# Attention beside a gated feed-forward network: the value products of two key tiles in one block, feed-forward products in six places of two rounds

## The chip, the cores and the metric

The kernel runs on one core of a Trainium2 chip. The core has five engines with queues of their own: TensorE (PE in the profile; its weight loads are shown apart as PEld), VectorE (DVE), ScalarE (ACT), GpSimd (POOL) and SyncE (SP), which here issues the DMAs. Each engine works through its own list of instructions in order and waits on semaphores for the others. TensorE writes only to PSUM, whose eight banks of 128 x 512 fp32 numbers have to be emptied by VectorE or ScalarE before they can be written again.

The metric is the device time of one execution in microseconds. Of the kernel before there are three runs: 1801.42, 1802.56 and 1802.78 us; the median is 1802.56.

## The reference

The input is one sequence of 2048 tokens with 512 features, all in fp32.

```
xn = layernorm(x)
q, k, v = split(xn @ wqkv)              # 32 heads of 16
p  = softmax(q @ k.T / sqrt(16))        # per head, 2048 x 2048
s  = (p @ v) @ wo
g  = silu(((xn @ w_gate) * (xn @ w_up)) @ w_down)   # inner width 1792
out = x + s * g
```

## The kernel before, in words

**Precision.** Most products run on TensorE as fp32r, a rounded fp32. To keep the accuracy, an operand is split into a high part and a low remainder, and a product is the sum of three (high times high, high times low, low times high). The value products alone run in plain fp32, which the chip does as two passes, so that each is two matmul records in the trace.

**Units, rounds, key tiles.** The attention is cut into 32 units: a group of four heads (eight groups) and a chunk of 512 query tokens (four chunks). A unit goes through 16 key tiles of 128 keys. One key tile of one unit is a *round*; the main loop runs over 512 rounds, `n` from 0 to 511, and `kt` is the key tile. In a round, for each of the four heads `j`:

- `expo` (line 603) multiplies the key tile by the queries into a PSUM tile `t` (keys on the partitions, 512 queries). Two further rows of the contraction carry the negated maximum of each query, so ScalarE's exponential (line 605) gives the unnormalised weights `e` in SBUF directly.
- `score` (line 578) makes the plain scores `s` (queries on the partitions, 512 keys) for a unit 21 rounds ahead (`LEAD`), and VectorE takes their maximum (line 580, `mx`). That is what `expo` of a later unit needs. The last 21 rounds have no scores.

The heads sit in the lower and the upper 64 partitions in turn: `t` of head `j` and `s` of head `j ^ 1` use different halves of the array's rows and run side by side. A `t` and its `s` are called a *pair* below; a round has four pairs, two rounds have eight.

**Value products.** `pv` (line 614) multiplies the `e` tiles of a round by the values and a column of ones (which gives the softmax's denominator), for its four heads in four strips of 32 output partitions of one PSUM bank, `pv`, accumulated over the 16 key tiles. They use all 128 rows of the array and 32 of its columns each, where the other products use 64 rows and 128 columns. After the last key tile, `finish` transposes, divides and sends the result out. The value products of a round are placed after the pairs of the next round.

**Feed-forward and projections.** The projections of queries and keys for later heads, the feed-forward network and the output projection are cut into products that run between the rounds' other work. `pair` (lines 256 to 277) makes two such outputs at a time, in two PSUM banks (`misc`), with the contraction cut into the lower and upper 64 rows: at each step one matmul of each half (lines 269 and 273), 24 or 30 steps in all, in two halves `k` = 0 and 1. It yields `k` and the number of steps ahead of each half, and then once a step. Between the halves ScalarE makes a one-element copy, `look`, that fixes the order. After a gate/up product ScalarE copies the gate out (`g`, line 374), VectorE multiplies it with the other output (`h`, line 376), and some steps later ScalarE and GpSimd split that into `hh` and `hl` (lines 334 and 335).

A `Filler` doles these steps out. It takes the step count of a half and the number of rounds that `spread` gives it (from `FFN_ROUNDS` = 484 rounds over all `SLOTS`), and in each round `part` issues an equal share of what is left. In the loop `part` is called once a round, after the second pair. So a round of TensorE's list is: pair, pair, four to six feed-forward steps, pair, pair, then the value products of the round before.

**What sets the order.** TensorE, ScalarE and VectorE keep exactly the order in which the program issues instructions (`manual_schedule`, `ORDERED`). `soon(n, fn)` puts small operations off by `n` calls of `step()`, which comes once after each pair. GpSimd and SyncE are ordered by a planner after the first 18 rounds.

**Buffers.** PSUM: `st` 2 banks for `t`, `s` 3, `pv` 1, `misc` 2 (`BUFS`). SBUF: 12 tiles for `e` (`EBUFS`), three for a unit's queries.

Of the kernel before, what the change touches and what calls it, by code (L numbers as in the profile page):

```python
# [21 lines left out]
NT = S // P  # L22
# [7 lines left out]
VCOLS = (H - 1) * VW + 32  # L30
THIRDS = [range(0, 5), range(5, 10), range(10, 14)]
LEAD = 21
FFN_ROUNDS = 484
SLOTS = 24 * (NC * (NG // 2 - 1) + 1) + 36 * NF * NC
SPLIT_ROUNDS = 4
EBUFS = 12
# [12 lines left out]
def body(ctx, tc, x, wqkv, wo, wg, wu, wd, out):  # L49
# [4 lines left out]
    class Tied:  # L54
# [3 lines left out]
        def __init__(self, engine):  # L58
            self.engine, self.last = engine, None
# [13 lines left out]
    def dma(dst, src):  # L73
        sync.dma_start(dst, src)
# [36 lines left out]
    def banks_of(bufs):  # L111
        stack = ExitStack()
        fst["ps"] = stack.enter_context(tc.tile_pool(name="ps" + "".join(bufs), bufs=1, space=PSUM, reuse_waits="tile")), bufs
        return stack

    def psum(tag, name):
        ps, bufs = fst["ps"]
        return ps.tile([P, 512], F32, tag=tag, name=name, bufs=bufs[tag])
# [290 lines left out]
    def o_split(c, tiles):  # L409

        for d, (oh, ol) in enumerate(tiles):
            heads = 8 if c < NC - 1 or d < ND - 1 else 4
            n = heads * DH
            raw = (wtile(("w1r", "w0r")[d]).rearrange("p d q -> p (d q)") if d < 2 else
                   fst["fp"].tile([P, D], F32, name="wdr", bufs=2))
            dma(raw[:n], OD[c][8 * d:8 * d + heads, 0:DH])
            pool.tensor_copy(oh[:n], raw[:n])
            pool.tensor_tensor(ol[:n], raw[:n], oh[:n], op=OP.subtract)
        ops[c] = now[0], tiles

    def small_tiles():

        return [[wtile(n + k).rearrange("p d q -> p (d q)") for k in "hl"] for n in ("w1", "w0") for _ in range(2)]

    def prepare():

        done = [(NG - 1) * NC + c in finished for c in range(NC)]
        if 0 not in ops:
            if done[0] and "w" in fst:
                o_split(0, small_tiles())  # L430
        for c in (1, 2):
            if c not in ops and done[c] and ("big", c) in fst:
                h, l = fst["big", c]
                o_split(c, [(h[:, d], l[:, d]) for d in range(ND)])
        if 3 not in ops and "first" in fst:
            o_split(3, small_tiles())
# [103 lines left out]
    NU = NG * NC  # L540
# [6 lines left out]
    def load_q(i):  # L547
        g, c = divmod(i, NC)
        QS[i] = q = keep.tile([P, 2, 512], F32R, name="qs", bufs=3)
        MX[i] = keep.tile([P, 4, 4, 4], F32, name="mx", bufs=2)  # L550
        for e in range(2):
            dmar(q[64 * e:64 * e + KB], two(QD[g // 2][c][64 * (g % 2):64 * (g % 2) + 64], e))

    def load_k(g, cs=range(NC)):
        heads = slice(64 * (g % 2), 64 * (g % 2) + 64)
        for e in range(2):
            k = ks[g % 2][64 * e:64 * e + KB]
            if g < 2:
                for c in cs:
                    dmar(k[:, :, c * 512:(c + 1) * 512], two(KD[0][c][heads], e))  # L560
            else:
                dmar(k, two(KD[g // 2][heads], e))
# [45 lines left out]
    def pv(i, kt, es):  # L608
        g = i // NC
        if kt == 0:  # L610
            fst["pv"] = psum("pv", f"pv{i}")
        for j in range(4):
            h0 = (4 * g + j) * VW
            nc.tensor.matmul(fst["pv"][32 * j:32 * j + 32], V[:, kt, h0:h0 + 32], es[j],  # L614
                             start=kt == 0, stop=kt == NT - 1)

    def finish(i):

        g, c = divmod(i, NC)
        tr = keep.tile([P, 16, 32], F32, name="tr", bufs=1)  # L620
        tn = tr.rearrange("p b e -> p (b e)")
        nc.vector.transpose(tn, fst["pv"])
        yield
        rc = keep.tile([P, 16, 1], F32, name="rc", bufs=1)
        nc.vector.reciprocal(rc, tr[:, :, DH:DH + 1])
        late = i >= NU - NC
        (nc.vector if late else pool).tensor_tensor(on[:, :, 0:DH], tr[:, :, 0:DH], rc.to_broadcast([P, 16, DH]),
                                                         op=OP.mult)
        for _ in range(1 if late else 5):
            yield  # L630
        nc.vector.transpose(tn, on.rearrange("p b e -> p (b e)"))
        if i == NU - 1:
            fst["tn"] = tn
            return
        dma(OD[c][4 * g:4 * g + 4], tn)
        finished.add(i)
# [111 lines left out]
    def filler(wq0):  # L748
        yield from proj_pair(0, [(wq0, 0, 2), (wq0, 0, 3)])
        for m in range(1, NG // 2):  # L750
            wk, wq = fst.get(("qk", m)) or (qk_weights(m, 1), qk_weights(m, 0))
            for c in range(NC):
                yield from proj_pair(m, [(wk, 1, c), (wq, 0, c)])
                if m == 1 and c:
                    after = fst["high"].ins.name
                    for n, src in enumerate((xh, xl)):
                        put = sync.dma_start(XD[c][n].bitcast(F32), src[c].bitcast(F32))
                        tc.add_manual_dep(put.ins, after, BEHIND, reason="not before the first exponentials")
                if m == NG // 2 - 1 and c == NC - 2:
                    nxt = gu_weights(0)  # L760
        flush()
        qkv.close()
        fst["fp"] = ffp.enter_context(tc.tile_pool(name="ffn", bufs=1, reuse_waits="tile"))
        yield from ffn(nxt)
# [3 lines left out]
    heads = []  # L768

    def step_small(q):  # L770
        if q and next(q[0], 1):
            q.pop(0)

    class Filler:


        def __init__(self, gen, rounds):
            self.gen, self.rounds = gen, rounds
            self.left = self.parts = 0
            self.done = False  # L780

        def fetch(self):
            v = next(self.gen, self)
            if v is self:
                self.done = True
            elif v:
                self.left, self.parts = v[1], self.rounds(v[1])

        def part(self):
            if not self.left and not self.done:  # L790
                self.fetch()
            if self.left:
                n = -(-self.left // self.parts)
                for _ in range(n):
                    next(self.gen)
                self.left -= n
                self.parts = max(1, self.parts - 1)
                if not self.left:
                    self.fetch()

    cum = [0]

    def spread(n):
        a = cum[0]
        cum[0] += n
        return max(1, round(cum[0] * FFN_ROUNDS / SLOTS) - round(a * FFN_ROUNDS / SLOTS))

    prev = None
    with tc.manual_schedule(engines=ORDERED):
        with banks_of(EARLY_BUFS):  # L810
            fil = Filler(filler(early()), spread)
        ctx.enter_context(banks_of(BUFS))
        for n in range(NU * 16):
            now[0] = n
            Tied.on = n < 18
            i, kt = divmod(n, 16)
            g, c = divmod(i, NC)
            si, sr = divmod(n + LEAD, 16)
            if kt == 8 and i + 2 < NU:
                load_q(i + 2)  # L820
            if kt == 0 and g + 1 < NG and c == 1:
                load_k(g + 1)
            es = []
            for j in range(4):
                es.append(expo(i, kt, j))
                if si < NU:
                    score(si, sr, j ^ 1)
                step()
                if j == 1:
                    prepare()  # L830
                    if fil.done:
                        fil = Filler(ending(), lambda n: 2)
                    fil.part()
            if sr == 15 and si < NU:
                maxima(si, 8 if si < NU - 1 else 4)
            step_small(heads)
            if kt % 4 == 2:
                soon(2, lambda: step_small(later))
            if prev is None:
                run(fst["v"])  # L840
            else:
                pv(*prev)
                if prev[1] == NT - 1:
                    heads.append(finish(prev[0]))
                    step_small(heads)
            prev = i, kt, es
        pv(*prev)
        run(finish(NU - 1))
        flush()
        last_heads()  # L850
        while fil.left or not fil.done:
            now[0] += 1
            prepare()
            fil.part()
            flush()
# [17 lines left out]
```

## Time and profile before

| | |
|---|---|
| median of three runs | 1802.56 us (1801.42 to 1802.78) |
| the profiled execution, its span | 1800.6 us |
| PE busy, matmuls | 1789.0 us (99%), 13578 |
| DVE busy | 1468.1 us (82%) |
| ACT busy | 1243.6 us (69%) |
| POOL busy | 572.9 us (32%) |
| exponentials (L605) | 2048, 596 ns each |
| maxima of the scores (L580) | 2048, 683 ns each |
| value matmuls (L614) | 4096, the first at 108.6 us, the last at 1785.0 us |

The profile is one execution, recorded by the hardware. The span runs from the first to the last instruction; the times of runs stand about 2 us above it. Busy time of PE is not useful work alone: the ends of matmuls are modelled, and matmuls overlap. What tells more is the start of one instruction against the start of the next, and for weight loads (PEld), exponentials and maxima what they waited for. A line of the timeline gives the start, the duration, the engine, the line of the kernel, the operation, output and inputs, the count, and in brackets the idle time of the engine before it and whose end closed that.

### The profile page before, as it was taken

How to read it: one execution, taken by the hardware profiler on the slowest of the kernel's cores; microseconds unless marked ns; L12 is line 12 of the kernel's file. 1: busy time of each engine (PE TensorE's matmuls, PEld its weight loads, DVE VectorE, ACT ScalarE, POOL GpSimd, SP SyncE). 2: the span in 40 equal slices, each digit the busy share in tenths (PEclk: the TensorE clock that was granted, in tenths of full speed). 3: DMA queues.
4: the chain of work that ended last, by engine and by line, in shares of the span. 5: the costliest groups of instructions: out<-in, count | busy, mean ns of one | idle time of the engine just before them, and what ended most of it. 6: DMA issues, size and time to landing. Idle time of an engine off the chain costs nothing.

```text
span 1800.6 us, 34192 instructions
## 1 busy us (share of the span) xinstructions
PE 1789.0 (99%) x13578; PEld 988.5 (55%) x13578; DVE 1468.1 (82%) x2440; ACT 1243.6 (69%) x2377; POOL 572.9 (32%) x639
## 2 busy tenths in 40 slices
PE   9999999999999999999999999999999999999998
PEld 5655555555555555555555555555555555555555
DVE  6778888888888888888888888888888888888832
ACT  6356676777776767777677777776767767777664
POOL 5312331532322324233132431431325323223350
PEclk9999999999999999999999999999999999999999
DMA  5317533511131122321024221411125111111352
GB/s 199 115 57 218 206 115 107 150 51 44 51 70 52 59 82 69 75 57 46 28 70 106 68 63 28 98 51 40 43 80 121 46 46 52 39 43 49 112 152 80
DMA packets 117227, 145.72 MB, mean 81 GB/s; under 512 B 12620, under 2 KB 74060, under 8 KB 114380
## 3 DMA queue, kind: packets, MB, share of 16 engines
q1 hardware_dynamic: 117068, 143.55, 27.4%
q8 instruction: 106, 1.74, 0.4%
q14 instruction: 53, 0.43, 0.1%
HBM read 95.94 MB, written 47.45 MB: 80 GB/s over the span
## 4 chain that ended last, share of the span: by engine, by line
PE 98%; ACT 1%; DVE 1%; POOL 0%; issue 0%; ACTq 0%; POOLq 0%; DVEq 0%
PE pv L614 28%; PE t L603 21%; PE s L578 12%; PE u L269 6%; PE y L269 5%; PE g L269 5%; PE u L273 4%; PE y L273 4%; PE g L273 2%; PE p L269 2%; PE v L250 2%; PE p L273 2%; PE z L269 1%; PE z L273 1%; PE p L250 1%; PE warm L668 1%
## 5 line engine op out<-in xcount | busy, mean ns | idle before, releaser
L580 DVE TENSOR_REDUCE mx<-s 128x1 f32<-128x512 f32 x2048 | 1310.7, 683 | 256.9 <-PE s L578 143.5
L605 ACT ACTIVATE e<-t 128x512 f32<-128x512 f32 x2048 | 1112.3, 596 | 427.7 <-PE s L578 257.7
L603 PE MATMUL t<-qs,ks 50*128 50x512 f32 x2048 | 707.9, 427 | 0.0
L578 PE MATMUL s<-ks,qs 48*128 48x512 f32 x2048 | 697.1, 427 | 0.8 <-DVE mx L580 0.8
L603 PEld LDWEIGHTS t<-qs,ks 50*128 50x128 f32 x2048 | 346.6, 184 | 499.6 <-ACT e L605 471.6
L614 PE MATMUL pv<-e,V 128*32 128x512 f32 x4096 | 545.7, 605 | 0.0
L578 PEld LDWEIGHTS s<-ks,qs 48*128 48x128 f32 x2048 | 336.7, 184 | 21.3 <-DVE mx L580 5.2
L63 POOL CAST w0h<-w0r 128x512 fp32r<-128x512 f32 x60 | 36.7, 611 | 415.7 <-PE u L269 251.9
L614 PEld LDWEIGHTS pv<-e,V 128*32 128x32 f32 x4096 | 81.0, 108 | 156.5 <-issue 147.0
L63 POOL CAST dh<-wdr 128x512 fp32r<-128x512 f32 x56 | 33.7, 613 | 183.3 <-PE y L273 114.0
L273 PE MATMUL y<-dh,hh 64*128 64x512 f32 x224 | 88.2, 394 | 0.0
L273 PE MATMUL u<-fh,w0h 64*128 64x512 f32 x224 | 88.2, 394 | 0.0
L269 PE MATMUL g<-fh,w1h 64*128 64x512 f32 x224 | 87.6, 391 | 0.0
L269 PE MATMUL u<-fl,w0h 64*128 64x512 f32 x224 | 87.5, 391 | 0.0
L269 PE MATMUL u<-fh,w0l 64*128 64x512 f32 x224 | 87.5, 390 | 0.0
L269 PE MATMUL g<-fh,w1l 64*128 64x512 f32 x224 | 87.5, 390 | 0.0
L273 PE MATMUL y<-dl,hh 64*128 64x512 f32 x224 | 87.4, 390 | 0.0
L269 PE MATMUL y<-dl,hh 64*128 64x512 f32 x224 | 87.4, 390 | 0.0
L269 PE MATMUL g<-fl,w1h 64*128 64x512 f32 x224 | 87.3, 390 | 0.0
L273 PE MATMUL y<-dh,hl 64*128 64x512 f32 x224 | 87.3, 390 | 0.0
L269 PE MATMUL y<-dh,hl 64*128 64x512 f32 x224 | 87.3, 390 | 0.0
L269 PE MATMUL y<-dh,hh 64*128 64x512 f32 x224 | 87.2, 389 | 0.0
(252 smaller groups left out, 2874.6 us busy)
## 6 DMA issues: line engine op xcount, KB each, us to landing
w1r<-in_wg_dram SPq DMA_DIRECT2D x56, 256.0 KB
w0r<-in_wu_dram SPq DMA_DIRECT2D x56, 256.0 KB
wdr<-in_wd_dram SPq DMA_DIRECT2D x56, 256.0 KB
qs<-QD SPq DMA_DIRECT2D x64, 192.0 KB
ks<-KD SPq DMA_DIRECT2D x12, 768.0 KB
KD<-hl SPq DMA_DIRECT2D x16, 512.0 KB
QD<-hl SPq DMA_DIRECT2D x16, 512.0 KB
OD<-tr SPq DMA_DIRECT2D x31, 256.0 KB
```

The lines of the kernel that those rows point to most:

```text
L63: got = getattr(self.engine, name)(*args, **kw)
L250: nc.tensor.matmul(o, l(d), r(d), start=k == d == 0, stop=k == 2 and d == ND - 1)
L269: nc.tensor.matmul(outs[k], l[LOWER], r[LOWER], start=k == 0 and n == 0, stop=(stop or k == 0) and n == len(low) - 1, skip_group_check=k == 1)
L273: nc.tensor.matmul(outs[1 - k], l[UPPER], r[UPPER], start=k == 0 and m == 0, stop=(stop or k == 0) and m == len(high) - 1, skip_group_chec ...
L578: nc.tensor.matmul(o, QS[i][b:b + KB, pr, t * P:(t + 1) * P], k[b:b + KB, pr, kc * 512:(kc + 1) * 512], start=True, stop=True)
L580: nc.vector.tensor_reduce(MX[i][:, j, t, kc:kc + 1], o, axis=AX.X, op=OP.max)
L603: nc.tensor.matmul(o, k[b:b + KR, pr, kt * P:(kt + 1) * P], QS[i][b:b + KR, pr], start=True, stop=True)
L605: nc.scalar.activation(e, o, AF.Exp, scale=DH ** -0.5)
L614: nc.tensor.matmul(fst["pv"][32 * j:32 * j + 32], V[:, kt, h0:h0 + 32], es[j], start=kt == 0, stop=kt == NT - 1)
L668: nc.tensor.matmul(psum("x", "warm"), ident, on.rearrange("p b e -> p (b e)"), start=True, stop=True)
```

## The change

The value products of two key tiles are issued together, after the four pairs of every second round. `prev` becomes a list: after the pairs of an even round, `values()` issues the value products of the two rounds before; the `e` tiles of three rounds are then in use. At the end of the loop the last two rounds are issued one by one.

The feed-forward steps are spread over six places in two rounds instead of one place in each. In an odd round (the first after a block of value products) the places are after the second, third and fourth pair, in an even round after the first, second and third (`GAPS`). The unit of `spread` becomes a cycle of two rounds (`CYCLES` = 240 instead of 484 rounds). `Filler` divides the 6 places of each cycle between the two halves of a product; where a half would begin in the middle of a cycle, it leaves its first place empty. A new product begins only at the first place of a cycle.

The numbers of matmuls, exponentials and maxima stay the same. So do the number of `st`, `s`, `pv` and `misc` banks and of `e` tiles.

```diff
-FFN_ROUNDS = 484
+CYCLES = 240
+GAPS = [(0, 1, 2), (1, 2, 3)]
...
             elif v:
-                self.left, self.parts = v[1], self.rounds(v[1])
-
-        def part(self):
-            if not self.left and not self.done:
+                k, self.left = v
+                if k == 0:
+                    self.gaps = 6 * self.cycles(2 * self.left)
+                    self.parts = self.gaps // 2
+                    self.gaps -= self.parts
+                else:
+                    self.skip = self.gaps % 6 != 0
+                    self.parts = self.gaps - self.skip
+
+        def part(self, first=True):
+            if first and not self.left and not self.done:
                 self.fetch()
-            if self.left:
+            if self.skip:
+                self.skip = 0
+            elif self.left:
...
-        return max(1, round(cum[0] * FFN_ROUNDS / SLOTS) - round(a * FFN_ROUNDS / SLOTS))
-
-    prev = None
+        return max(1, round(cum[0] * CYCLES / SLOTS) - round(a * CYCLES / SLOTS))
+
+    prev = []
+
+    def values():
+        for p in prev:
+            pv(*p)
+            if p[1] == NT - 1:
+                heads.append(finish(p[0]))
+                step_small(heads)
+        prev.clear()
...
                 if j == 1:
                     prepare()
+                if n and j in GAPS[n % 2]:
                     if fil.done:
                         fil = Filler(ending(), lambda n: 2)
-                    fil.part()
+                    fil.part(n % 2 and j == 1)
...
-            if prev is None:
+            if n == 0:
                 run(fst["v"])
-            else:
-                pv(*prev)
-                if prev[1] == NT - 1:
-                    heads.append(finish(prev[0]))
-                    step_small(heads)
-            prev = i, kt, es
-        pv(*prev)
+            elif n % 2 == 0 or n == NU * 16 - 1:
+                values()
+            prev.append((i, kt, es))
+        pv(*prev[0])
```

More of the change, by code (lines that the diff above doesn't have):

```diff
@@ L774, in body, with __init__ @@
     class Filler:
-        def __init__(self, gen, rounds):
-            self.gen, self.rounds = gen, rounds
-            self.left = self.parts = 0
+        def __init__(self, gen, cycles):
+            self.gen, self.cycles = gen, cycles
+            self.left = self.parts = self.gaps = self.skip = 0
             self.done = False
```

## The prediction

> **What bounds the kernel now.** I read the page first: busy shares, clock, the chain that ended last, and the costliest groups.
>
> ```profile
> span 1800.6 us, 34192 instructions
> PE 1789.0 (99%) x13578; PEld 988.5 (55%) x13578; DVE 1468.1 (82%) x2440; ACT 1243.6 (69%) x2377; POOL 572.9 (32%) x639
> PEclk9999999999999999999999999999999999999999
> PE 98%; ACT 1%; DVE 1%; POOL 0%; issue 0%; ACTq 0%; POOLq 0%; DVEq 0%
> L580 DVE TENSOR_REDUCE mx<-s 128x1 f32<-128x512 f32 x2048 | 1310.7, 683 | 256.9 <-PE s L578 143.5
> L605 ACT ACTIVATE e<-t 128x512 f32<-128x512 f32 x2048 | 1112.3, 596 | 427.7 <-PE s L578 257.7
> L603 PEld LDWEIGHTS t<-qs,ks 50*128 50x128 f32 x2048 | 346.6, 184 | 499.6 <-ACT e L605 471.6
> ```
>
> TensorE is on the chain for 98% of the span, at full clock. But its 99% is no measure of useful work: a matmul's modelled end covers the time until the next starts. The last line is the hint: weight loads of the exponential scores `t` stood idle 471.6 us until an exponential `e` had ended. So I read one round instruction by instruction (columns: start, duration, engine, line, operation, count, idle time before it and what ended that).
>
> ```profile
> 547.59 1.07 PE L614 MATMUL pv<-e,V 128*32 128x512 f32 x8
> 548.59 0.18 PEld L603 LDWEIGHTS t<-qs,ks 50*128 50x128 f32 x1 [0.84 <-ACT e L605]
> ...
> 548.93 0.40 PE L603 MATMUL t<-qs,ks 50*128 50x512 f32 x1
> ...
> 549.12 1.09 ACT L605 ACTIVATE e<-t 128x512 f32<-128x512 f32 x2 [0.62 <-PE s L578]
> ...
> 549.40 0.39 PE L269 MATMUL y<-dl,hh 64*128 64x512 f32 x1
> ...
> 549.63 0.40 PE L269 MATMUL y<-dh,hl 64*128 64x512 f32 x1
> ...
> 549.77 0.18 PEld L603 LDWEIGHTS t<-qs,ks 50*128 50x128 f32 x1 [0.18 <-ACT e L605]
> ...
> 549.87 0.40 PE L603 MATMUL t<-qs,ks 50*128 50x512 f32 x1
> ...
> 550.26 0.18 PEld L603 LDWEIGHTS t<-qs,ks 50*128 50x128 f32 x1 [0.30 <-ACT look L277]
> ...
> 550.30 1.09 ACT L605 ACTIVATE e<-t 128x512 f32<-128x512 f32 x2
> 550.69 1.06 PE L614 MATMUL pv<-e,V 128*32 128x512 f32 x8
> ```
>
> The `t` products have two PSUM banks, so the third of a round can only load once the first exponential has ended, and the fourth after the second. Here they do: the first exponential ends at 549.12 + 0.60 = 549.72 and the third load starts at 549.77; the second ends at 549.12 + 1.09 = 550.21 and the fourth starts at 550.26 (the profile names `look`, a one-element copy that ended beside it and touches none of these banks). This round has three feed-forward steps (a step is a pair of matmuls on the two halves of the array's rows; 549.40 to 549.63: 0.23 us each; 24 steps make a gate/up product, 30 or 24 a down-projection product). Rounds with six and four steps follow, the starts of the value blocks (the 0.64 is cut off by the edge of the stretch asked for):
>
> ```profile
> 351.53 1.07 PE L614 MATMUL pv<-e,V 128*32 128x512 f32 x8
> 355.04 1.07 PE L614 MATMUL pv<-e,V 128*32 128x512 f32 x8
> 358.15 1.06 PE L614 MATMUL pv<-e,V 128*32 128x512 f32 x8
> ...
> 367.87 0.64 PE L614 MATMUL pv<-e,V 128*32 128x512 f32 x4
> ...
> 400.34 1.07 PE L614 MATMUL pv<-e,V 128*32 128x512 f32 x8
> ...
> 439.71 1.06 PE L614 MATMUL pv<-e,V 128*32 128x512 f32 x8
> ```
>
> Six steps take 3.51, four 3.11, and three took 3.10 above as well. So a light round is already set by ScalarE's answer through the two banks, a heavy one by TensorE's own work. A gate/up product over its five rounds takes 367.87 - 351.53 = 16.34; two down-projection products over twelve rounds of five steps (first and last of thirteen block starts) take 39.37.
>
> **The reckoning.** Count from a round's first `t`. Let E be the time at which a pair of `t` and score really starts.
> - E1 = 0.10 (the first weight load is bare after the block: exponential at 0.53 after it, but 0.43 after the third `t`, 549.87 to 550.30). E2 = 0.34.
> - The next pair follows 0.23 later, plus 0.23 for each feed-forward step between.
> - An exponential starts 0.43 after its pair, no sooner than 0.49 (1.09 - 0.60) after the one before, and lasts 0.60.
> - The pair after next starts no sooner than 0.15 after that end (0.05 to the load, 0.10 from load to matmul). So E3 is at least 1.28 and E4 1.77; later each is at least 1.18 (0.43 + 0.60 + 0.15) after the one two before.
> - The value block starts 0.33 after the last E (550.69 - 550.36) and lasts 1.00.
>
> This gives 3.51 for six steps (E3 1.95, E4 2.18) and 3.10 for four or three (E4 1.77 by the banks), as measured.
>
> **The change, part by part.** (a) *Half the value blocks.* One block costs beside its pure stream: 0.33 instead of 0.23 on entry (0.10), 0.14 for its first weights and its end (1.00 less two passes of 0.43), 0.34 instead of 0.23 for the pair after (0.11). That is 0.35 us for each block saved, 89 us over 255, if nothing else holds TensorE.
>
> What a second key tile costs in a block is seen once before, at the end of the loop:
>
> ```profile
> 1783.33 2.25 PE L614 MATMUL pv<-e,V 128*32 128x512 f32 x16
> L614 PE MATMUL pv<-e,V x7: 592/592/592, 1783.8 to 1784.2; 128*32 128x512 f32 x7
> ```
>
> The passes start 0.4 apart; I take 0.43, so 0.86 for a tile (0.90, twice the first pass's 0.45, is the other end: 1.06 less 0.61; 0.04 x 255 = 10 us). The block becomes 1.00 + 0.86 = 1.86.
>
> (b) *What the blocks covered.* The two `t` banks stay, and each block hides two exponentials. Before, every four exponentials had a block; now eight have one. A waiting `t` load holds up all behind it on TensorE: its score, the next feed-forward steps, and so the next maximum on VectorE. With E8 followed by 0.33 + 1.86 = 2.19, the kinds of two-round cycle come out so (steps in the six places; counted in the written-out order of TensorE's instructions):
> - 2,2,2,2,2,2 (108 cycles): E = 0.10, 0.34, 1.28, 1.97, 2.66, 3.35, 4.04, 4.73; length 6.92. Only E3 waits, by 0.25.
> - 1,1,1, none, 2,2 (48): 0.10, 0.34, 1.28, 1.77, 2.46, 2.95, 3.64, 4.33; 6.52.
> - 2,2,2,1,1,1 (41) and 2,2,1,1,1,1 (35): E8 4.33 by the banks; 6.52.
> - 2,2,2,2,2,1 (13): 6.72. Even with no steps 6.32, above two light rounds of before (6.20).
>
> Two gate/up (or projection) products fill five cycles: 2 x 6.92 + 3 x 6.52 = 33.40 against 2 x 16.34 = 32.68, +0.36 each. 69 of these and 8 small down-projection products: 77 x 0.36 = +27.7. Two large down-projection products: 2 x (6.92 + 6.52 + 6.72) = 40.32 against 39.37, eight times: +7.6.
>
> The Trainium skill, "TensorEngine Tiling (Array Packing)", says two things of this. By Key Properties a change of tiling mode drains TensorE: the trace agrees with the 0.35 us of (a), and by that rule alone the time is the first rival's. By Performance Considerations, PSUM Bottleneck, a faster TensorE leaves the emptying of PSUM as it was: the trace agrees with the 0.18 us wait at 549.77, and by that rule the time is the forecast.
>
> (c) *ScalarE's own order.* Three operations stand among the exponentials:
>
> ```profile
> L334 ACT ACTIVATE hh<-h 128x512 fp32r<-128x512 f32 x56 | 35.4, 633 | 0.0
> L374 ACT ACTIVATE g<-g 128x512 f32<-128x512 f32 x56 | 33.5, 598 | 19.6 <-PE u L269 15.4 <-PE g L273 1.8
> L277 ACT ACTIVATE look<-u 1x1 f32<-1x1 f32 x56 | 9.0, 160 | 15.2 <-PE u L273 12.5
> ```
>
> The copy `g` now falls between the seventh and eighth exponential of a cycle; the 1.86 block hides it (uncovered, 0.5 x 56 = 28). The split `hh` falls right behind the third, pushes the fourth by about 0.5, and so E6: +0.1 where the cycle has two steps everywhere, +0.3 in 2,2,2,1,1,1, half each: 0.2 x 56 = +11. `look` comes where a half product ends, ahead of the eighth exponential or in a stretch that waits for a bank anyway: nothing (bounds 0 to 0.16 x 56 = 9).
>
> (d) *At nothing.* The twelve `e` tiles are then all in use before a block; its first half frees four, and the next exponential comes after it. The `pv` bank is read between blocks a whole cycle apart. The three score banks: a maximum takes 0.68, less than the 0.69 between pairs of a heavy cycle; where the `t` banks allow 0.59, VectorE falls behind by 0.1 a pair, half a microsecond in all, which the third bank holds and the block makes good. Each of its other operations follows the eighth score into the block. SP issues the same 567 instructions, ScalarE 2380; VectorE two fewer, GpSimd two more; the three weight loads of a product move with it by a round or less, and GpSimd is 32% busy. The last ten cycles have no scores; I take them as even, between the change of a heavy cycle (6.92 against twice 3.51) and a light one (6.52 against twice 3.10): -1 to +3.
>
> Sum: 27.7 + 7.6 + 11 = +46 on the span of 1800.6, so 1847; the median of the runs, 1802.56, stands 2.0 above that span: 1849. Own range, from the ends above (value tile, `hh` 0 to 17, `look`, tail): 1828 to 1875.
>
> **Rivals.**
> 1. *Only TensorE's stream counts* (faster). No pair waits for a bank; the cycles are 6.67, 5.52, 5.98, 5.75 and 6.44: two products 30.59 (-1.05 each, x 77 = -81), two large ones 37.26 (-2.11 x 8 = -17): 1705. For it: TensorE is 98% of the chain, and each block has its 0.35. Against: rounds with three and four steps take the same 3.10. It decides if the third `t` of a cycle loads sooner than an exponential after the block.
> 2. *The wait is paid once a cycle*, at E3, and ScalarE then keeps to its 0.49: +0.25 on rival 1 a cycle, +0.48 where one step stands in the first place; two products 32.07 (-0.30 x 77), large ones -0.15 x 8: about -25, 1778. Against: the 1.18 in two steps has no slack to lose.
> 3. *ScalarE's short operations land in the way every cycle*, 0.15 more on 254 cycles: 1887. For it: it waits 12.5 us for TensorE ahead of `look`, in order, exponentials behind.
>
> **How the numbers follow.** Forecast 0.74, rivals 0.06, 0.07 and 0.13. The range 1820 to 1890 leaves out the first two and a little of the ends. Within 0.2% (about what a measurement can tell) is 0.02, between the forecast and the second rival; slower 0.86, faster 0.12.
>
> **What would show it.** Right: after a block the third `t` loads some 1.18 after the first, with an exponential as what ended its wait; cycles of 6.9 and 6.5; one block of 1.86 in each; TensorE still called busy 99%. Wrong, if cycles of 5.5 to 6.0 appear, if a score's load waits for a maximum, or if value weights wait in the middle of a block.

## The result and the profile after

The changed kernel takes 1857.8 us (median; 1857.12 to 1858.61) against 1802.45 of the kernel before (a fourth run, 1802.34, has joined the three named above): 1.0308 times the time, 95% interval 1.0294 to 1.0323. It is slower. The forecast was 1849, with 1820 to 1890 as its range. The profiled execution has a span of 1855.5, 54.9 more than the 1800.6 before.

From the page of the changed kernel (lines of the kernel are one higher than before: 604 is `expo`, 579 `score`, 615 `pv`):

```profile
span 1855.5 us, 34207 instructions
PE 1825.2 (98%) x13578; PEld 976.1 (53%) x13578; DVE 1474.1 (79%) x2438; ACT 1268.8 (68%) x2377; POOL 574.4 (31%) x641
PE 92%; ACT 6%; DVE 1%; issue 1%; POOL 0%; DMA 0%; ACTq 0%; POOLq 0%; DVEq 0%
L606 ACT ACTIVATE e<-t 128x512 f32<-128x512 f32 x2048 | 1161.5, 597 | 510.2 <-PE s L579 262.1
L604 PEld LDWEIGHTS t<-qs,ks 50*128 50x128 f32 x2048 | 357.0, 184 | 510.4 <-ACT e L606 330.0
```

TensorE still counts as busy 98% of the span, with the same 13578 matmuls: of the added 54.9 us, 36.2 stand as busy time (1825.2 against 1789.0), though the work is the same, since a matmul's modelled end can reach over a wait. The chain of waits shows more: ScalarE has 6% of it, where it had 1%. Neither of the engines that empty PSUM is near its limit: VectorE fell from 82% to 79%, ScalarE from 69% to 68%.

The starts of six value blocks (timeline, TensorE; start, duration, and so on; the last is cut off by the edge of the stretch asked for):

```profile
802.99 1.92 PE L615 MATMUL pv<-e,V 128*32 128x512 f32 x16
809.97 1.92 PE L615 MATMUL pv<-e,V 128*32 128x512 f32 x16
816.94 1.92 PE L615 MATMUL pv<-e,V 128*32 128x512 f32 x16
823.78 1.92 PE L615 MATMUL pv<-e,V 128*32 128x512 f32 x16
830.34 1.92 PE L615 MATMUL pv<-e,V 128*32 128x512 f32 x16
836.87 0.64 PE L615 MATMUL pv<-e,V 128*32 128x512 f32 x4
```

These are five cycles with two gate/up products: two cycles of twelve steps (6.98 and 6.97), then 2,2,2,1,1,1 (6.84), 1,1,1, none, 2,2 (6.56) and 2,2,1,1,1,1 (6.53). Together 33.88, where two such products took 2 x 16.34 = 32.68 before. Inside the second:

```profile
811.83 0.18 PEld L604 LDWEIGHTS t<-qs,ks 50*128 50x128 f32 x1 [0.84 <-issue]
...
812.17 0.39 PE L604 MATMUL t<-qs,ks 50*128 50x512 f32 x1
812.36 4.58 ACT L606 ACTIVATE e<-t 128x512 f32<-128x512 f32 x7 [1.68 <-PE s L579]
813.01 0.18 PEld L604 LDWEIGHTS t<-qs,ks 50*128 50x128 f32 x1 [0.41 <-ACT e L606]
...
813.81 0.40 PE L604 MATMUL t<-qs,ks 50*128 50x512 f32 x1
...
816.61 0.40 PE L604 MATMUL t<-qs,ks 50*128 50x512 f32 x1
...
816.94 0.64 PE L615 MATMUL pv<-e,V 128*32 128x512 f32 x4
```

The block that began at 809.97 ends with the next `t` load at 811.83: 1.86 for two key tiles, 0.14 less than two blocks of 1.00, and the pairs then follow 0.34 apart. The value side of the change does what it should. But the third `t` loads at 813.01, 1.18 after the first and 0.05 after the end of the first exponential (812.36 + 0.60 = 812.96). TensorE had finished the steps ahead of it; ScalarE had waited 1.68 us for work and its answer came too late.

### The profile page after: what moved, and what is told of

Its sections match the earlier page's. It is cut to its first block, busy times and chain, and to the rows that moved or that the text cites. A ratio compares the mean times of both kernels' runs of the same rounds, so it can differ in the third digit from the quotient of the medians.

```text
span 1855.5 us, 34207 instructions
## 1 busy us (share of the span) xinstructions
PE 1825.2 (98%) x13578; PEld 976.1 (53%) x13578; DVE 1474.1 (79%) x2438; ACT 1268.8 (68%) x2377; POOL 574.4 (31%) x641
## 4 chain that ended last, share of the span: by engine, by line
PE 92%; ACT 6%; DVE 1%; issue 1%; POOL 0%; DMA 0%; ACTq 0%; POOLq 0%; DVEq 0%
PE pv L615 26%; PE t L604 25%; PE s L579 9%; PE u L270 5%; PE y L270 5%; PE g L270 4%; ACT e L606 4%; PE g L274 3%; PE u L274 3%; PE y L274 3%; PE v L251 2%; PE p L274 2%; PE z L270 2%; PE p L270 2%; ACT hh L335 1%; PE p L251 1%
## 5 line engine op out<-in xcount | busy, mean ns | idle before, releaser
L606 ACT ACTIVATE e<-t 128x512 f32<-128x512 f32 x2048 | 1161.5, 597 | 510.2 <-PE s L579 262.1
L604 PE MATMUL t<-qs,ks 50*128 50x512 f32 x2048 | 850.0, 436 | 18.3 <-ACT e L606 16.2
L579 PE MATMUL s<-ks,qs 48*128 48x512 f32 x2048 | 831.6, 436 | 0.8 <-DVE mx L581 0.8
L615 PE MATMUL pv<-e,V 128*32 128x512 f32 x4096 | 493.8, 600 | 0.0
L579 PEld LDWEIGHTS s<-ks,qs 48*128 48x128 f32 x2048 | 349.1, 184 | 22.0 <-issue 5.0
L615 PEld LDWEIGHTS pv<-e,V 128*32 128x32 f32 x4096 | 107.1, 109 | 235.0 <-issue 226.5
L64 POOL TENSOR_TENSOR hl<-h,hh 128x512 fp32r<-128x512 f32 x56 | 72.2, 1290 | 76.8 <-ACT hh L335 74.1
L274 PE MATMUL u<-fh,w0l 64*128 64x512 f32 x224 | 88.0, 393 | 0.0
L270 PE MATMUL g<-fh,w1l 64*128 64x512 f32 x224 | 87.8, 392 | 0.0
L274 PE MATMUL g<-fh,w1l 64*128 64x512 f32 x224 | 87.8, 392 | 0.0
L270 PE MATMUL y<-dh,hl 64*128 64x512 f32 x224 | 87.8, 392 | 0.0
L270 PE MATMUL u<-fh,w0l 64*128 64x512 f32 x224 | 87.7, 392 | 0.0
```

The lines of the kernel that those rows point to most:

```text
L64: got = getattr(self.engine, name)(*args, **kw)
L270: nc.tensor.matmul(outs[k], l[LOWER], r[LOWER], start=k == 0 and n == 0, stop=(stop or k == 0) and n == len(low) - 1, skip_group_check=k == 1)
L274: nc.tensor.matmul(outs[1 - k], l[UPPER], r[UPPER], start=k == 0 and m == 0, stop=(stop or k == 0) and m == len(high) - 1, skip_group_chec ...
L579: nc.tensor.matmul(o, QS[i][b:b + KB, pr, t * P:(t + 1) * P], k[b:b + KB, pr, kc * 512:(kc + 1) * 512], start=True, stop=True)
L604: nc.tensor.matmul(o, k[b:b + KR, pr, kt * P:(kt + 1) * P], QS[i][b:b + KR, pr], start=True, stop=True)
L606: nc.scalar.activation(e, o, AF.Exp, scale=DH ** -0.5)
```

## The experiments

The theory: with two PSUM banks for `t`, a pair can start only 0.15 after the exponential of the pair two before, and a block of value products covers two exponentials, whatever its length. The rivals: TensorE's stream alone decides; or the wait is paid once a cycle; or there is some cost of the double block or of the six places in themselves.

**Half-wide exponentials, in both kernels.** If ScalarE's answer is what holds TensorE, an exponential of half the length should turn the loss into a gain. The value products then read the 256 columns twice, so both versions leave out half of the exponentials and are no longer the reference's softmax.

```diff
-        nc.scalar.activation(e, o, AF.Exp, scale=DH ** -0.5)
-        return e
+        nc.scalar.activation(e[:, 0:256], o[:, 0:256], AF.Exp, scale=DH ** -0.5)
+        return e[:, 0:256].rearrange("p (a q) -> p a q", a=1).to_broadcast([P, 2, 256])
...
-            nc.tensor.matmul(fst["pv"][32 * j:32 * j + 32], V[:, kt, h0:h0 + 32], es[j],
+            nc.tensor.matmul(fst["pv"][32 * j:32 * j + 32].rearrange("p (a q) -> p a q", a=2), V[:, kt, h0:h0 + 32], es[j],
```

In the kernel before:

> The kernel before with each exponential on 256 of the 512 columns; the value products read these 256 twice, so the right half of the weights is a copy of the left and the softmax is not the reference's. TensorE's list is unchanged. An exponential should last about 0.38 us (0.16 for one element, 0.60 for 512: 0.16 + half of 0.44; an estimate). Bank theory: the fourth t of a light round no longer waits (E4 1.72 instead of 1.77), 240 light rounds lose 0.04 each, heavy rounds nothing: 1792, within 1785 to 1800. If ScalarE does not matter: 1802.

In the changed kernel:

> The changed kernel with the same half-wide exponentials (same change to the computation). Bank theory: the third t now needs E3 = 0.10 + 0.43 + 0.38 + 0.15 = 1.06 against 1.03 from the stream, and a pair may follow the one two before after 0.96 instead of 1.18; cycles of 6.70 (12 steps), 6.05, 6.05 and 5.86: two gate/up products 31.4, about 40 us less than the half-wide kernel before, so 1745 to 1765: the change turns from a loss into a gain. If the double block or the six places cost TensorE themselves (a rival: the block is dearer than 1.86, or steps beside scores run slower), the loss of 55 us stays: 1845 to 1860.

Measured: 1790.95 in the kernel before (0.9932 of it, interval 0.9918 to 0.9947) and 1761.14 in the changed one (0.9768, 0.9752 to 0.9784). With the short exponential the same change gains 30 us (about 40 was expected) instead of losing 55. From the changed kernel with it, the page's group of the exponentials:

```profile
L606 ACT ACTIVATE e<-t 128x256 f32<-128x256 f32 x2048 | 757.4, 383 | 797.6 <-PE s L579 443.8
```

And five block starts around the same kinds of cycle (12 steps, then the three lighter ones; the last line is cut off):

```profile
802.91 1.92 PE L615 MATMUL pv<-e,V 128*32 128x512 f32 x16
809.65 1.93 PE L615 MATMUL pv<-e,V 128*32 128x512 f32 x16
815.76 1.92 PE L615 MATMUL pv<-e,V 128*32 128x512 f32 x16
821.97 1.92 PE L615 MATMUL pv<-e,V 128*32 128x512 f32 x16
828.23 1.07 PE L615 MATMUL pv<-e,V 128*32 128x512 f32 x8
```

The exponential takes 383 ns, as estimated, and the cycles 6.74, 6.11, 6.21 and 6.26 instead of 6.97, 6.84, 6.56 and 6.53. Over the whole run the medians of these four kinds are 6.76, 6.11, 6.20 and 5.98; the 6.26 is an unusual cycle of its kind, in which VectorE also transposes the values of a finished unit (0.72 at 823.96) and the last score's load waits for a maximum. So the loss does not lie in the double block or the six places as such: with them unchanged, a quicker ScalarE turns it round.

**Three banks for `t`, two for the scores,** in the changed kernel.

```diff
-BUFS = {"st": 2, "s": 3, "pv": 1, "misc": 2}
+BUFS = {"st": 3, "s": 2, "pv": 1, "misc": 2}
```

> The changed kernel with three PSUM banks for the t products and two for the scores. If two t banks are the only thing in the way, the third pair starts at 1.03 and the time falls well below 1800. My theory counts VectorE's banks the same way: a maximum takes 0.68 and the next but one score has to wait for it, so E3 = 0.56 + 0.68 + 0.15 = 1.40 instead of 1.28, and in light cycles the pairs follow at 0.65 or so instead of 0.59: +0.12 for a heavy, +0.25 for a light cycle on the changed kernel, 1885 to 1915.

Measured: 1904.49 (1.0564 of the kernel before, 1.0546 to 1.0582), inside the range of the theory. A cycle that begins with the load at 815.36, and the row of who waited for whom (total us, times, longest):

```profile
815.36 0.18 PEld L604 LDWEIGHTS t<-qs,ks 50*128 50x128 f32 x1 [0.84 <-issue]
...
816.17 0.40 PE L604 MATMUL t<-qs,ks 50*128 50x512 f32 x1
816.68 0.18 PEld L579 LDWEIGHTS s<-ks,qs 48*128 48x128 f32 x1 [0.55 <-DVE mx L581]
...
PEld s L579 <- DVE mx L581: 140.4, 440, 2.5
```

The third `t` now runs at 0.81, without a wait; its score loads only at 1.32, when VectorE has emptied the first of two banks. The wait is handed from ScalarE to VectorE.

**Each part of the change alone.** First the double blocks with the feed-forward steps in one place a round, as before (lines of the edit against the changed kernel; `Filler`, `spread` and `FFN_ROUNDS` are again those of the kernel before):

```diff
...
-                if n and j in GAPS[n % 2]:
...
-                    fil.part(n % 2 and j == 1)
+                    fil.part()
```

> Value products of two key tiles in one block, feed-forward steps in one place a round as in the kernel before. Bank theory: the fifth and sixth pair follow the fourth at once and wait for banks (E5 = E3 + 1.18): 4 and 4 steps 6.52, 6 and 6 steps 7.39, 4 and 6 6.98, 6 and 4 6.93, 5 and 5 6.93. With 80, 50, 36, 35 and 37 such cycles the loop is some 75 to 85 us longer than before: 1875 to 1890, dearer than the whole change. If only the stream counts: 0.35 less for each block saved, about 1715.

Measured: 1963.76 (1.0892, 1.0876 to 1.0908), far above the expectation. The direction was the theory's, the size not. The timeline of a 4 and 4 cycle whose first load is at 902.89 shows why (line numbers as in the kernel before):

```profile
904.38 0.40 PE L603 MATMUL t<-qs,ks 50*128 50x512 f32 x1
...
904.64 0.42 PE L603 MATMUL t<-qs,ks 50*128 50x512 f32 x1
904.82 2.27 ACT L605 ACTIVATE e<-t 128x512 f32<-128x512 f32 x4 [0.31 <-PE s L578]
905.46 0.18 PEld L603 LDWEIGHTS t<-qs,ks 50*128 50x128 f32 x1 [0.72 <-ACT e L605]
...
905.95 0.18 PEld L603 LDWEIGHTS t<-qs,ks 50*128 50x128 f32 x1 [0.30 <-ACT e L605]
```

The third and fourth pair run 0.26 apart, but their exponentials follow each other at 0.49. I had used that spacing in the prediction and left it out here: the fourth exponential starts at 2.42, not 2.20, so the sixth pair starts at 3.16 instead of 2.95 (3.06 + 0.10 measured), and everything behind it moves. With the rule the cycles are 6.73 (4 and 4), 7.19 (5 and 5) and 7.65 (6 and 6); measured were medians of 6.76, 7.19 and 7.66. So most of the miss was an error of mine in using the theory. Not all of it: with the rule the loss comes to an estimated 138 us (the ruled lengths of the five kinds against rounds of 3.10, 3.28 and 3.51, by the counts of the expectation), and 161 were measured. Cycles of 4 and 6 steps and of 6 and 4 took 7.28 and 7.23 in the median where the rule gives 7.19; the rest was not followed up.

Then the six places with value products in every round:

```diff
-            elif n % 2 == 0 or n == NU * 16 - 1:
+            else:
                 values()
```

> Feed-forward steps in six places of two rounds as in the changed kernel, value products in every round as before. Bank theory: in the odd round the third pair has only two steps or fewer ahead of it and waits to 1.28, and the steps behind the fourth pair cover nothing: 3.76 for the odd and 3.50 for the even heavy round (7.26 against 7.02), 6.63 to 6.86 for the light ones (against 6.20 to 6.61). About 95 us longer: 1885 to 1905. If only the stream counts, the same work in another order: 1795 to 1805.

Measured: 1916.77 (1.0632, 1.0616 to 1.0648), 12 above the expected range. Four block starts, around a light round (one step in each place), a heavy odd and a heavy even one:

```profile
803.43 1.06 PE L615 MATMUL pv<-e,V 128*32 128x512 f32 x8
806.53 1.06 PE L615 MATMUL pv<-e,V 128*32 128x512 f32 x8
810.31 1.06 PE L615 MATMUL pv<-e,V 128*32 128x512 f32 x8
813.83 1.06 PE L615 MATMUL pv<-e,V 128*32 128x512 f32 x8
```

3.10, 3.78 and 3.52, where 3.10, 3.76 and 3.50 were reckoned. Over the run, light even rounds take the 3.10 as reckoned; the 155 odd rounds of six steps average 3.84 and the 102 even ones 3.53, which is some 16 of the 19 us between the 95 expected and the 114 measured. Why 19 of the odd ones take 4.0 and more was not followed up. The work was the same as before in another order, so the order alone cost 114 us here. Alone, the blocks cost 161 and the places 114; together 55. The parts are no sum: by the theory, the places put steps where the double block leaves pairs waiting.

**ScalarE's split of `h` ahead of the block,** in the changed kernel.

```diff
-                    soon(4, lambda h=h, hi=hh[:, i], lo=hl[:, i]: hidden(h, hi, lo))
+                    soon(1, lambda h=h, hi=hh[:, i], lo=hl[:, i]: hidden(h, hi, lo))
```

> The changed kernel with ScalarE's split of h moved from behind the third exponential of the next cycle to behind the eighth of the same one, ahead of the value block. It pushed the fourth exponential by 0.5 there, +0.1 in 28 heavy cycles and +0.3 in 28 others; now the block covers it: 11 us less than the changed kernel, 1843 to 1851. If it was hidden anyway: no change from 1858.

Measured: 1846.66 (1.0244, 1.0228 to 1.0259), 11 less than the changed kernel, as the prediction's term said. In the changed kernel's 6.84 cycle above (first load at 818.79) one sees what it did:

```profile
821.01 0.62 ACT L335 ACTIVATE hh<-h 128x512 fp32r<-128x512 f32 x1
...
821.53 2.95 ACT L606 ACTIVATE e<-t 128x512 f32<-128x512 f32 x5
822.17 0.18 PEld L604 LDWEIGHTS t<-qs,ks 50*128 50x128 f32 x1 [0.49 <-ACT e L606]
```

The fourth exponential starts at 821.53, and the sixth `t`, which needs its bank, waits 0.49 and starts at 3.48. Over the run, the cycles of 2,2,2,1,1,1 that held the split take 6.86 in the median in the changed kernel and 6.55 here, those of twelve steps 7.07 and 6.98.

**The same steps where the waits are.** If the third pair waits until 1.28 in any case, three steps ahead of it cost nothing; and in light cycles steps can be dealt so that each fills a wait.

```diff
+PLANS = {(24, 2): ([3, 2, 2, 2, 2, 1], [3, 2, 2, 2, 2, 1]),
+         (24, 3): ([3, 1, 1, 1, 1, 1, 3, 1], [0, 1, 2, 1, 3, 1, 1, 1, 1, 1]),
+         (30, 3): ([3, 1, 2, 1, 2, 1, 3, 2], [0, 2, 2, 1, 3, 1, 2, 1, 2, 1])}
...
-                n = -(-self.left // self.parts)
+                n = self.plan.pop(0) if self.plan else -(-self.left // self.parts)
```

> The changed kernel with the same steps per cycle but put where the banks make TensorE wait: three steps ahead of the third pair, then 2,2,2,2,1 in cycles of twelve; 3,1,1,1,1,1 and 3,1,0,1,2,1 in cycles of eight; 3,1,2,1,2,1 in cycles of ten. Bank theory: three steps ahead of the third pair end at 1.26, under its 1.28, so a cycle of twelve takes 6.69 instead of 6.92, and cycles of eight and ten the floor of 6.32 instead of 6.52. The split of h still costs 0.13 or 0.50 where it falls (+18 us). Together 1808, within 1795 to 1820. If the waits are not at these places: no change from 1858.

Measured: 1813.91 (1.0061, 1.0046 to 1.0076), inside the expected range and 44 less than the changed kernel. And with the split of `h` ahead of the block as well:

> The same plan with the split of h ahead of the block as well: 18 us less than the plan alone, 1790, within 1780 to 1800, and so below the kernel before.

Measured: 1795.14 (0.9963, 0.9948 to 0.9977): 0.4% less than the kernel before, a small difference, with no change outside its interval, 5 us above the expected 1790, and the only version with the full computation that beats both kernels. Its block starts (line 618 is `pv` here):

```profile
801.11 1.92 PE L618 MATMUL pv<-e,V 128*32 128x512 f32 x16
807.47 1.92 PE L618 MATMUL pv<-e,V 128*32 128x512 f32 x16
813.79 1.92 PE L618 MATMUL pv<-e,V 128*32 128x512 f32 x16
820.54 1.92 PE L618 MATMUL pv<-e,V 128*32 128x512 f32 x16
827.31 1.93 PE L618 MATMUL pv<-e,V 128*32 128x512 f32 x16
833.64 1.92 PE L618 MATMUL pv<-e,V 128*32 128x512 f32 x16
```

Cycles of eight steps take 6.36, 6.32 and 6.33, those of twelve 6.75 and 6.77; 6.32 and 6.69 were reckoned. Cycles of ten (3,1,2,1,2,1) take 6.34 in the median, the same as eight.

## Why the prediction was right

**(a) The blocks.** Right in place and size: 1.86 for two key tiles, 0.33 ahead of it (816.94 - 816.61) and 0.34 for the pair after it. The bound of 0.90 for the second tile was not needed. The Trainium skill, "TensorEngine Tiling (Array Packing)", Key Properties, says that a change of tiling mode drains TensorE. The trace agrees as far as a block still costs 0.10, 0.14 and 0.11 us beside its stream, now once for two key tiles; it does not tell a drain from weights that load in the open. By that rule alone the kernel would have got faster, and with the half-wide exponential it did.

**(b) What the blocks covered.** This was the step that decided. The third `t` loads 1.18 after the first, with an exponential as what ended the wait. Cycles without the split of `h` took 6.97 (twelve steps), 6.54 to 6.55 (seven to nine) and 6.75 (eleven) in the median, where 6.92, 6.52 and 6.72 were forecast. The half-wide exponential, the swap of banks and the dealt steps each tested it from another side. The second rule of the Trainium skill that the prediction cites, from "TensorEngine Tiling (Array Packing)", PSUM Bottleneck, is that tiling speeds up TensorE but not the emptying of PSUM. The measured time agrees with it, in the form that the runs show here: not the throughput of ScalarE, 68% busy, but its answer through two banks held TensorE.

**(c) ScalarE's own order.** 11 us forecast, 11 measured by taking it out; +0.10 in twelve-step cycles and +0.31 in those of 2,2,2,1,1,1, as reckoned. `look` and `g` needed no term: twelve-step cycles with `g` alone take 6.97 in the median, with `look` alone 6.98, with no such operation 6.96. But the list of three operations was not complete. The 16 tanh operations of the silu (line 341) stand on ScalarE's list too:

```profile
L341 ACT ACTIVATE e<-y 128x512 f32<-128x512 f32 x16 | 10.1, 633 | 0.0
```

A twelve-step cycle with one of them and the split takes 7.37 instead of 7.07, one of 2,2,2,1,1,1 with both 7.16 instead of 6.86. Against other cycles of their kind the cycles with these sixteen are some 4 us longer in all; the prediction had no term for them.

**(d) At nothing.** VectorE's banks held: loads of scores waited for a maximum 4.4 us in all, and 5.2 in the kernel before.

**The size.** 46 us were forecast on the span, 54.9 came. Up to 4 of the 9 missing are the silu's operations. The rest is a small undersize of the cycles: pairs with two steps between them follow at 0.70 where 0.69 was reckoned, and the medians are 0.02 to 0.05 above the forecast in cycles without the split. I set reckoned cycles after against measured rounds before, but that is little of it: the reckoning gives 16.32 for the five rounds that took 16.34, and reckoned against reckoned would have forecast 48 us. How much each of these has of the 9 is not settled.

**The rivals.** *Only TensorE's stream* is out: in the changed kernel its light cycles of 5.5 to 6.0 appear nowhere, and no cycle with scores is under 6.32. *The wait is paid once a cycle* is out too: it makes cycles of seven and eight steps 6.00 long, and both took 6.55. The later waits were there, as in the cycle whose first `t` loads at 825.63 (its third and fifth load of `t`):

```profile
826.82 0.18 PEld L604 LDWEIGHTS t<-qs,ks 50*128 50x128 f32 x1 [0.65 <-ACT e L606]
...
828.01 0.18 PEld L604 LDWEIGHTS t<-qs,ks 50*128 50x128 f32 x1 [0.40 <-ACT e L606]
```

*ScalarE's short operations in every cycle* is out as well: only the split of `h` and the silu's tanh cost, and only in the cycles where they fell.

**A reading that was too large.** I took the 471.6 us of idle `t` loads ended by an exponential as the hint. In the kernel before with half-wide exponentials, where nearly no bank wait is left, the same row is still there (total, times, longest):

```profile
PEld t L603 <- ACT e L605: 427.1, 509, 1.1
```

That is the 0.84 after each of the value blocks, in which no weights of a `t` are loaded anyway and which the profile puts to the exponential that had ended last. About 45 of the 471.6 were waits for a bank. The hint pointed the right way by its name and not by its size; the single round, read row by row, carried the argument.

## What to carry to other kernels

Merging blocks of one engine's work saves its switches, but it also merges the cover that each block gave to another engine's latency: reckon how many results the waiting engine can hand back per block through the buffers it has, before counting the switches saved. Where a fixed wait per cycle remains, put independent work exactly ahead of it rather than evenly: here the same steps dealt by the waits, and one ScalarE copy moved under the block, turned +3.1% into -0.4%. A busy share of 98 or 99% with no change in the count of matmuls says nothing on such waits; start-to-start times of one cycle do.

## What the runs showed that was not expected

That each part of the change would cost more alone than both together was expected; that the double blocks alone would cost 161 us, and not some 80, was not. Nor were the silu's sixteen tanh operations, which lengthen single cycles by 0.1 to 0.3 us. The swap of one bank between `t` and the scores came out as expected, and shows how evenly the two were matched: with three banks for `t`, weight loads of the scores at once stood idle for 140 us in 440 waits.
